# A linear-attention block and an FFN on one core: Q by seven block products, some of them among the K/V tiles

## The chip, the core and the metric

The kernel runs on one core of a Trainium2 chip. The metric is the device time of one execution in microseconds; the time before is the median of three runs.

## The reference

Two blocks read the same layer-normalised input `xn` (2048 tokens, 1024 features), and the second gates the first.

```python
xn = layernorm(x)                                   # (1, 2048, 1024), no scale or bias
q, k, v = split_heads(xn @ wqkv)                    # 32 heads of 32
phi = lambda t: where(t > 0, t + 1, exp(t)) + 1e-6
pq, pk = phi(q), phi(k)
kv = einsum("bhsd,bhse->bhde", pk, v)               # one 32x32 matrix a head, over all tokens
z  = pk summed over the tokens
o  = (pq @ kv) / (pq . z + 1e-6)
s  = o @ wo
g  = silu((silu(xn @ w_gate) * (xn @ w_up)) @ w_down)
return x + s * g
```

K and V of all 2048 tokens must be known before the first `o`; Q is needed only from there on.

## The kernel before

**Layout.** Tokens go in 16 tiles of 128 rows (`i`), in 4 blocks of 512 (`b`) and, in the FFN, in 2 passes of 1024 (`p`). `xnT[p]` holds `xn` transposed, features on the partitions, in fp16. The first 8 tiles are transposed by PE (`emit_T`, L305), blocks 2 and 3 through DRAM with a DMA transpose (`emit_A2_block`, L341).

**K and V.** `emit_B(i, c)` (L375) multiplies one token tile with a chunk of 512 columns of the K/V weights, 8 matmuls of 128x512; chunks 0 and 1 are K, chunks 2 and 3 are V. `emit_phi` (L123) makes phi of a 512-wide chunk in fp32: an exp and a relu on ACT, an addition of 1e-6 on Pool or DVE (L128), and min and add in one DVE instruction (L129). `emit_C(i)` (L379) adds the tile's `pk`-by-`v` products into three PSUM tiles `kvz`, 8 small matmuls.

**Q.** `emit_Q(b, g)` (L144) is one group of 128 output features for one block: 8 matmuls of 128x512 (L150) and an `emit_phi` into `pqT`. There are 4 x 8 groups, so 256 matmuls.

**Output of the attention.** `emit_ND(b, t)` (L510) multiplies `pqT` with the masked `KVZ`, 8 small matmuls into three PSUM tiles, and divides on DVE. When the four tiles of a block are done, `emit_OT(b)` (L537) stores the block to `o_dram` in one DMA and reads it back with a DMA transpose into `oT`. `emit_S(b, t, cc)` (L543) multiplies with `wo`, 8 matmuls of 128x512 each, 32 such calls.

**Order.** Up to tile 2 an order written by hand holds for PE, DVE, ACT and Pool. After that a scheduler places the instructions, in about the order of the source: all eight Q groups of block 0 after the last K/V tile, then a queue `fq` gives two pieces of work (L563) after every `emit_ND`: the Q groups of blocks 1 to 3 first, then `emit_S` of the blocks that are through. PSUM has three buffers for `psA` (`kvz`, later `nd_ps`), three for `psB` (`kv_ps`, `q_ps`, `s_ps`) and two for `psC`.

**FFN.** Each of its groups is a 2x2 block product done with seven products of half size, 28 matmuls instead of 32. `Group` (L608) runs it in parts: `part_a` (M3 into X, M4 into Y), `part_b` (M1 into Z, M5 onto X, M2 onto Y), `part_c` (N7 onto X, N6 onto Y); ACT copies X, and DVE makes the running sum u and the two differences u - X and u - Y. The operands are sums of blocks of `xnT` (five of them a pass, `xs`, L750) and of the weights (`sum_w`, L761). The first `sum_w` calls stand inside the FFN's own order.

Of the kernel before, what the change touches and what calls it, by code (L numbers as in the profile page):

```python
# [21 lines left out]
def kernel(  # L22
# [37 lines left out]
    PE_T_BLOCKS = min(2, NB)  # L60
# [10 lines left out]
    wgu = ctx.enter_context(tc.tile_pool(name="wgu", bufs=4, side=RIGHT))  # L71
    ps12 = ExitStack()
    psA = ps12.enter_context(tc.tile_pool(name="psA", bufs=3, space=PSUM))
    psB = ps12.enter_context(tc.tile_pool(name="psB", bufs=3, space=PSUM))
    psC = ps12.enter_context(tc.tile_pool(name="psC", bufs=2, space=PSUM))
# [40 lines left out]

    def blk_rows(t_dram, b):
        return t_dram[b * TB:(b + 1) * TB, :]
# [4 lines left out]
    def emit_phi(work, t_ps, dst, W, eng=None):  # L123
        e_t = work.tile([P, W], FP32, name="e_t", tag="e_t")
        ex = nc.scalar.activation(out=e_t[:], in_=t_ps, func=ACT.Exp)
        r_t = work.tile([P, W], FP32, name="r_t", tag="r_t")
        nc.scalar.activation(out=r_t[:], in_=t_ps, func=ACT.Relu)  # L127
        (eng or nc.vector).tensor_scalar(out=r_t[:], in0=r_t[:], scalar1=EPS, scalar2=None, op0=ALU.add)  # L128
        nc.vector.scalar_tensor_tensor(out=dst, in0=e_t[:], scalar=1.0, in1=r_t[:],  # L129
                                       op0=ALU.min, op1=ALU.add)  # L130
        return ex

    p12 = ExitStack()
    wqp = p12.enter_context(tc.tile_pool(name="wqp", bufs=1))
    blk12 = p12.enter_context(tc.tile_pool(name="blk12", bufs=3))
    wop = p12.enter_context(tc.tile_pool(name="wop", bufs=1))
    phiw = p12.enter_context(tc.tile_pool(name="phiw", bufs=3))

    wq_sb = wqp.tile([P, DC, D], BF16, name="wq_sb")
    wo_sb = wop.tile([P, G, D], BF16, name="wo_sb")  # L140

    pqT_tiles = {}

    def emit_Q(b, g):  # L144
        if b not in pqT_tiles:
            pqT_tiles[b] = blk12.tile([P, G, TB], BF16, name="pqT", tag="pqT")
        pqT = pqT_tiles[b]
        q_ps = psB.tile([P, TB], FP32, name="q_ps", tag="B")
        for dc in range(DC):
            nc.tensor.matmul(q_ps[:], lhsT=wq_sb[:, dc, g * P:(g + 1) * P], rhs=xn_blk_ap(b)[:, dc, :],  # L150
                             start=(dc == 0), stop=(dc == DC - 1))
        emit_phi(phiw, q_ps[:], pqT[:, g, :], TB)
# [846 lines left out]
```

## Time and profile before

| what | value |
|---|---|
| median of the runs | 766.86 us (766.53 to 766.88) |
| profiled execution, its own time | 767.05 us |
| its span (first to last instruction) | 765.3 us |
| PE busy | 753.2 us, 98% of the span |
| DVE busy | 481.3 us, 63% |
| ACT busy | 271.5 us, 35% |
| Pool busy | 81.1 us, 11% |
| first FFN matmul of the profiled execution | 251.32 us |

The profiled execution is 1.75 us longer than its span and 0.19 us longer than the median. A matmul of 512 columns shows as 379 ns, but matmuls are pipelined; how closely they follow each other is read from the start of one run of matmuls to the start of the next. A line of the timeline gives the start, the duration of the merged instructions, the engine, the source line, the operation, the tiles, the count and, in brackets, the idle time of that engine just before it with what ended it. In lines of groups the last columns are busy time, mean duration of one instruction, and idle time before them.

### The profile page before, as it was taken

Reading aid. Unit: us, or ns where it says so; the run is one execution under the profiler, and the core shown is the slowest. Engines: PE = TensorE matmul, PEld = TensorE weight load, DVE = VectorE, ACT = ScalarE, POOL = GpSimd, SP = SyncE. Lnnn points to the kernel's source line nnn. Section 1 sums busy time; section 2 is a strip of 40 time slices with the busy share of each in tenths; the row PEclk is TensorE's granted clock in tenths of the full one; section 3 lists DMA queues with packets and bytes.
Section 4 is the critical chain, followed back from the end, with each engine's and each line's share of the span. In section 5 each row is a group of like instructions: output and inputs, shape, how many; then the busy total and the mean of one; then the engine's idle time right before and its main releaser. Section 6 shows DMA issues by size and latency. Waiting matters only on the chain.

```text
span 765.3 us, 9974 instructions
## 1 busy us (share of the span) xinstructions
PE 753.2 (98%) x3760; PEld 354.8 (46%) x3796; DVE 481.3 (63%) x955; ACT 271.5 (35%) x473; POOL 81.1 (11%) x89
## 2 busy tenths in 40 slices
PE   9999999999999999999999999999999999999997
PEld 3445444455544444444444444444444444444454
DVE  7777112699760677677876778767655654455454
ACT  3444444555333443433334333334433111111111
POOL 3133434000000000000000000000000221212220
PEclk9999999999999999999999999999999999999999
DMA  9545362015561155553555535453959944454300
GB/s 319 179 144 171 69 150 70 1 56 150 167 193 69 51 150 158 158 172 96 166 151 154 170 104 173 144 144 106 319 179 331 363 180 179 179 174 148 118 28 27
DMA packets 127087, 115.98 MB, mean 152 GB/s; under 512 B 28864, under 2 KB 107840, under 8 KB 125760
## 3 DMA queue, kind: packets, MB, share of 16 engines
q1 hardware_dynamic: 126752, 114.97, 47.8%
q8 instruction: 29, 0.48, 0.3%
q10 hardware_dynamic: 288, 0.39, 0.1%
q14 instruction: 18, 0.15, 0.1%
HBM read 70.52 MB, written 38.54 MB: 143 GB/s over the span
## 4 chain that ended last, share of the span: by engine, by line
PE 95%; DVE 3%; issue 1%; POOL 0%; ACT 0%; DVEq 0%
PE X L605 28%; PE Y L605 28%; PE kv_ps L359 12%; PE Z L605 9%; PE q_ps L150 7%; PE s_ps L551 7%; DVE stats L245 1%; PE nd_ps L523 1%; PE w_ps L401 1%; PE kvz L383 1%; PE tr_ps L312 0%; DVE pk_sb L129 0%; DVE xnT L332 0%; DVE mv L260 0%; POOL lnw L288 0%
## 5 line engine op out<-in xcount | busy, mean ns | idle before, releaser
L605 PEld LDWEIGHTS <-ws_all 128*128 128x128 bf16 x1260 | 122.0, 98 | 145.7 <-DVE ws_all L764 1.7
L625 DVE TENSOR_TENSOR q<-n,Y 128x512 f32<-128x512 f32 x63 | 43.3, 687 | 133.6 <-PE Y L605 132.7
L359 PE MATMUL kv_ps<-wkv_sb,xnT 128*128 128x512 bf16 x499 | 113.4, 379 | 2.2 <-ACT r_t L127 1.0
L932 POOL TENSOR_TENSOR o_out<-y,xres 128x512 bf16<-128x512 f32 x28 | 34.1, 1218 | 576.8 <-DVE y L931 576.8
L605 PEld LDWEIGHTS <-xs 128*128 128x128 bf16 x616 | 57.9, 98 | 63.2
L359 PEld LDWEIGHTS <-xnT 128*128 128x128 f16 x512 | 49.0, 98 | 57.9 <-issue 1.6
L605 PE MATMUL Y<-xs,ws_all 128*128 128x512 f16 (+3 forms) x308 | 70.3, 360 | 0.0
L605 PE MATMUL X<-xnT,ws_all 128*128 128x512 f16 (+1 forms) x278 | 70.1, 379 | 0.2
L605 PE MATMUL Z<-xs,ws_all 128*128 128x512 f16 x224 | 57.5, 379 | 1.2 <-DVE ws_all L764 1.2
L605 PE MATMUL Y<-xnT,ws_all 128*128 128x512 f16 x224 | 57.5, 379 | 0.0
L605 PE MATMUL X<-xs,ws_all 128*128 128x512 f16 x224 | 57.5, 379 | 0.0
L150 PE MATMUL q_ps<-xnT,wq_sb 128*128 128x512 f16 x256 | 57.3, 379 | 0.0
L551 PE MATMUL s_ps<-wo_sb,oT 128*128 128x512 bf16 x250 | 55.7, 379 | 0.3
L129 DVE SCALAR_TENSOR_TENSOR pk_sb<-e_t,r_t 128x512 bf16<-128x512 f32 x32 | 21.9, 688 | 54.2 <-POOL r_t L128 54.1
L784 ACT ACTIVATE g<-cg 128x512 bf16<-128x512 f32 x56 | 35.3, 630 | 54.3 <-DVE cg L640 54.3
L631 DVE TENSOR_TENSOR u<-Z,q 128x512 f32<-128x512 f32 x63 | 43.2, 686 | 15.7 <-PE Z L605 15.7
L784 ACT ACTIVATE g<-X 128x512 bf16<-128x512 f32 x28 | 16.7, 597 | 101.3 <-PE X L605 101.3
L128 POOL TENSOR_SCALAR r_t<-r_t 128x512 f32<-128x512 f32 x26 | 39.4, 1517 | 71.1 <-ACT r_t L127 60.9
L621 ACT COPY n<-X 128x512 f32<-128x512 f32 x63 | 36.9, 585 | 28.4 <-PE X L605 28.4
L809 DVE TENSOR_TENSOR ho<-g,up 128x1024 bf16<-128x1024 bf16 x56 | 38.2, 686 | 0.5
L551 PEld LDWEIGHTS <-oT 128*128 128x128 bf16 x256 | 24.8, 98 | 29.1
L150 PEld LDWEIGHTS <-wq_sb 128*128 128x128 bf16 x256 | 24.5, 98 | 27.2
(124 smaller groups left out, 979.3 us busy)
## 6 DMA issues: line engine op xcount, KB each, us to landing
h_dram<-ho SPq DMA_DIRECT2D x56, 256.0 KB, 2.5
wg_sb<-in_B_w_gate_dram SPq DMA_DIRECT2D x14, 512.0 KB, 4.1
wu_sb<-in_B_w_up_dram SPq DMA_DIRECT2D x14, 512.0 KB, 4.6
wdr<-in_B_w_down_dram SPq DMA_DIRECT2D x14, 512.0 KB, 4.1
ws_all<-h_dram SPq DMA_DIRECT2D x4, 1792.0 KB, 8.7
wds_dram<-wdsA SPq DMA_DIRECT2D x14, 384.0 KB, 2.8
hp_a<-h_dram SPq DMA_DIRECT2D x3, 1792.0 KB, 8.8
o_dram<-o_blk SPq DMA_DIRECT2D x4, 1024.0 KB, 4.6
```

Source lines behind the costliest of these rows:

```text
L128: (eng or nc.vector).tensor_scalar(out=r_t[:], in0=r_t[:], scalar1=EPS, scalar2=None, op0=ALU.add)
L129: nc.vector.scalar_tensor_tensor(out=dst, in0=e_t[:], scalar=1.0, in1=r_t[:], op0=ALU.min, op1=ALU.add)
L150: nc.tensor.matmul(q_ps[:], lhsT=wq_sb[:, dc, g * P:(g + 1) * P], rhs=xn_blk_ap(b)[:, dc, :], start=(dc == 0), stop=(dc == DC - 1))
L359: mm = nc.tensor.matmul(kv_ps[:], lhsT=xn_tok_ap(i)[:, dc, :], rhs=wkv_sb[:, dc, c * CW:(c + 1) * CW], start=(dc == 0), stop=(dc == DC - 1))
L551: nc.tensor.matmul(s_ps[:], lhsT=oT[:, c, ttok], rhs=wo_sb[:, c, cc * CW:(cc + 1) * CW], start=(c == 0), stop=(c == G - 1))
L605: marks["mm"] = nc.tensor.matmul(acc[:, 0:c1 - c0], lhsT=lhs(k), rhs=rhs(k)[:, c0:c1], start=(first and k == 0), stop=(k == n - 1), skip_g ...
L621: nc.scalar.copy(out=n[:], in_=self.X[:])
L625: nc.vector.tensor_tensor(out=self.q[:], in0=n[:], in1=self.Y[:], op=ALU.add)
L631: nc.vector.tensor_tensor(out=self.u[:], in0=Z[:], in1=self.q[:], op=ALU.add)
L784: nc.scalar.activation(out=self.g[:, i, j * TB:(j + 1) * TB], in_=src, func=ACT.Silu)
L809: nc.vector.tensor_tensor(out=self.ho[:, i], in0=self.g[:, i], in1=self.up[:, i], op=ALU.mult)
L932: (nc.vector if last else nc.gpsimd).tensor_tensor(out=self.o_out[:, i, cs], in0=t[:], in1=self.xres[:, i, cs], op=ALU.add)
```

## The change

Q is made by the FFN's method. `QGroup(p, m)` stands for 256 output features and 1024 tokens: 28 matmuls in parts a, b and c as in the FFN, and a part d for phi. There are 4 groups in each of 2 passes, so 224 matmuls. The sums `xs` of both passes and the sums of the Q weights are made earlier, spread among the K/V tiles by a queue `later`. The groups of pass 0 stand inside the K/V tiles 9, 11, 13 and 15; those of pass 1 follow after the last K/V tile, with the four `emit_ND` of block 0 among them.

Phi becomes bf16 and 1024 wide: exp and relu write bf16 tiles `e_t` and `r_t` of 1024 columns from the pool `phiw` (three buffers each), and `emit_phi(eng, ...)` is one tensor_scalar (min with 1, add 1e-6) and one tensor_tensor. It runs on DVE, except for the second row of each group of pass 1, which goes to Pool. In the built program all four of these second rows of pass 1 lie at the same address (`e_t` and `r_t` alike).

PSUM has five buffers for `psB` and none for `psC`. The `xn` tiles, the Q groups' outputs `pqT` and the transposed `o` of blocks 2 and 3 take memory that the FFN's sums, the weight buffers and `wq_sb` use at other times. A block's `o` is stored by tile, four DMAs, before the DMA transpose. An order written by hand now holds on PE, DVE, ACT and Pool up to the FFN; SP's is still set by the scheduler. The FFN's first weight sums stand among the last `emit_S`. The FFN itself is not changed.

```diff
-    psB = ps12.enter_context(tc.tile_pool(name="psB", bufs=3, space=PSUM))
-    psC = ps12.enter_context(tc.tile_pool(name="psC", bufs=2, space=PSUM))
+    psB = ps12.enter_context(tc.tile_pool(name="psB", bufs=5, space=PSUM))
...
+    def xsum_ops(p):
+        b11, b12 = xnT[p][:, 0:HD, 0:TB], xnT[p][:, 0:HD, TB:2 * TB]
+        b21, b22 = xnT[p][:, HD:DC, 0:TB], xnT[p][:, HD:DC, TB:2 * TB]
+        return [lambda k=k, u=u, v=v, op=op: nc.vector.tensor_tensor(out=XS[p][:, k], in0=u, in1=v, op=op)
+                for k, (u, v, op) in enumerate(((b21, b11, ALU.subtract), (b12, b22, ALU.subtract), (b11, b22, ALU.add),
+                                                (b21, b22, ALU.add), (b11, b12, ALU.add)))]
...
+    def block_operands(w, ws):
+        ws = ws.rearrange("p (k c) -> p k c", k=HD)
+        return {"M4": lambda k: w[:, HD + k, P:2 * P], "M3": lambda k: w[:, k, 0:P],
+                "M1": lambda k: ws[:, k, 0:P], "M5": lambda k: ws[:, k, P:2 * P], "M2": lambda k: ws[:, k, 2 * P:3 * P],
+                "N7": lambda k: ws[:, k, 3 * P:4 * P], "N6": lambda k: ws[:, k, 4 * P:5 * P]}
...
+    def emit_exp_relu(e, r, t):
+        nc.scalar.activation(out=e, in_=t, func=ACT.Exp)
+        nc.scalar.activation(out=r, in_=t, func=ACT.Relu)
+    def emit_phi(eng, dst, e, r):
+        eng.tensor_scalar(out=e, in0=e, scalar1=1.0, scalar2=EPS, op0=ALU.min, op1=ALU.add)
+        return eng.tensor_tensor(out=dst, in0=e, in1=r, op=ALU.add)
...
-    def emit_Q(b, g):
-        if b not in pqT_tiles:
-            pqT_tiles[b] = blk12.tile([P, G, TB], BF16, name="pqT", tag="pqT")
-        pqT = pqT_tiles[b]
-        q_ps = psB.tile([P, TB], FP32, name="q_ps", tag="B")
-        for dc in range(DC):
-            nc.tensor.matmul(q_ps[:], lhsT=wq_sb[:, dc, g * P:(g + 1) * P], rhs=xn_blk_ap(b)[:, dc, :],
-                             start=(dc == 0), stop=(dc == DC - 1))
-        emit_phi(phiw, q_ps[:], pqT[:, g, :], TB)
+    phiw = p12.enter_context(tc.tile_pool(name="phiw", bufs=3))
...
+    def phi_tiles():
+        return (phiw.tile([P, SP_TOK], BF16, name="e_t", tag="e_t"), phiw.tile([P, SP_TOK], BF16, name="r_t", tag="r_t"))
...
+    class QGroup:
+        def __init__(self, p, m, eng1):
+            w = wq_sb[:, :, m * FW:(m + 1) * FW]
+            self.lhs, self.rhs = block_operands(w, ws_all[:, m // 2, m % 2]), x_operands(p)
+            self.eng = (nc.vector, eng1)
+            self.out = wgu.tile([P, 2, SP_TOK], BF16, name="pqT", tag=("wg_sb" if m % 2 == 0 else "wu_sb"))
+            pqT_tiles[(p, m)] = self.out
+            self.row = {}
+        def mm(self, acc, which, first):
+            products(acc, self.lhs[which], self.rhs[which], HD, first)
...
+        def er(self, i, j):
+            if i not in self.row:
+                self.row[i] = phi_tiles()
+            return tuple(t[:, j * TB:(j + 1) * TB] for t in self.row[i])
+        def part_a(self):
+            self.X = psB.tile([P, CW], FP32, name="qX", tag="B")
+            self.mm(self.X, "M3", True)
+            self.u = qtmp.tile([P, CW], FP32, name="qu", tag="qu")
+            nc.scalar.copy(out=self.u[:], in_=self.X[:])
+            self.Y = psB.tile([P, CW], FP32, name="qY", tag="B")
+            self.mm(self.Y, "M4", True)
+            nc.vector.tensor_tensor(out=self.u[:], in0=self.u[:], in1=self.Y[:], op=ALU.add)
+        def part_b(self):
+            Z = psB.tile([P, CW], FP32, name="qZ", tag="B")
+            self.mm(Z, "M1", True)
+            nc.vector.tensor_tensor(out=self.u[:], in0=self.u[:], in1=Z[:], op=ALU.add)
+            self.mm(self.X, "M5", False)
+            emit_exp_relu(*self.er(0, 1), self.X[:])
+            self.mm(self.Y, "M2", False)
+            emit_exp_relu(*self.er(1, 0), self.Y[:])
+        def part_c(self):
+            for acc, which, i in ((self.X, "N7", 0), (self.Y, "N6", 1)):
+                self.mm(acc, which, False)
+                e, r = self.er(i, i)
+                nc.vector.tensor_tensor(out=r, in0=self.u[:], in1=acc[:], op=ALU.subtract)
+                emit_exp_relu(e, r, r)
+        def part_d(self):
+            for i in range(2):
+                emit_phi(self.eng[i], self.out[:, i, :], *(t[:] for t in self.row[i]))
...
+    ET = mybir.EngineType
+    FRONT_ORDER = {ET.PE, ET.DVE, ET.Activation, ET.Pool}
...
+        def emit_B_out(i, c):
+            kv_ps = kv_tiles.pop((i, c))
+            if c < NCC:
+                if c == 0:
+                    er_tiles[i] = phi_tiles()
+                emit_exp_relu(*(t[:, c * CW:(c + 1) * CW] for t in er_tiles[i]), kv_ps[:])
+                if c == NCC - 1:
+                    pk_tiles[i] = work.tile([P, D], BF16, name="pk_sb", tag="pk_sb")
+                    emit_phi(nc.vector, pk_tiles[i][:], *(t[:] for t in er_tiles.pop(i)))
...
+        later = deque()
+        for b in range(2, NB):
+            for t in range(TPB):
+                later.append(lambda i=b * TPB + t: emit_stats(i, parts=(0,)))
+                later.append(lambda i=b * TPB + t: (emit_stats(i, parts=(1,)), emit_aggr(i)))
+            later.append(lambda i=b * TPB: emit_rstd(i))
+            if b > 2:
+                for t in range(TPB):
+                    later.append(lambda b=b, t=t: emit_norm(b * TPB + t, xn_blk_slot(b)[:, t, :]))
+                later.append(lambda b=b: emit_xT_block(b))
+            else:
+                norm_b2 = [lambda b=b, t=t: emit_norm(b * TPB + t, xn_blk_slot(b)[:, t, :]) for t in range(TPB)]
+                norm_b2.append(lambda b=b: emit_xT_block(b))
+        pos = 2 * TPB + 1 + 4
+        later = deque(list(later)[:pos] + norm_b2 + list(later)[pos:])
+        later.extend(xsum_ops(0))
+        for m in range(NM_Q):
+            later.extend(wsum_ops(wq_sb[:, :, m * FW:(m + 1) * FW], ws_all[:, m // 2, m % 2]))
+        later.extend(xsum_ops(1))
...
+        with tc.manual_schedule(engines=FRONT_ORDER):
...
+            Q0 = 2 * TPB + 1
+            qp0 = deque(range(NM_Q))
+            for i in range(TPB, NT):
+                grp = QGroup(0, qp0.popleft(), nc.vector) if i >= Q0 and (i - Q0) % 2 == 0 and qp0 else None
+                nf = 1 if grp else 2
+                emit_B(i, 0)
+                fill(nf)
+                emit_C(i - 1)
+                if grp:
+                    grp.part_a()
+                emit_B(i, 1)
+                fill(nf)
+                if grp:
+                    grp.part_b()
+                if i == TPB:
+                    emit_T(TPB + 2)
+                emit_B(i, 2)
+                fill(nf)
+                if i == TPB:
+                    emit_T(TPB + 3)
+                if grp:
+                    grp.part_c()
+                emit_B(i, 3)
+                if grp:
+                    grp.part_d()
+                fill(nf)
+            emit_C(NT - 1)
...
+            nc.sync.dma_start(out=o_dram[r0:r0 + P, :], in_=o_sb[:])
+            if t == TPB - 1:
+                nc.sync.dma_start_transpose(out=oT_of(b), in_=blk_rows(o_dram, b))
...
+        with tc.manual_schedule(engines=FRONT_ORDER):
+            qs = [QGroup(NPASS - 1, m, nc.gpsimd) for m in range(NM_Q)]
+            qs[0].part_a()
+            emit_KVZ()
+            qs[0].part_b()
+            emit_ND(0, 0)
+            for m in range(1, NM_Q):
+                qs[m].part_a()
+                qs[m - 1].part_c()
+                emit_ND(0, m)
+                qs[m - 1].part_d()
+                qs[m].part_b()
+            qs[-1].part_c()
+            qs[-1].part_d()
+            nd = deque((b, t) for b in range(1, NB) for t in range(TPB))
+            ns = 0
+            for b in range(NB):
+                for t in range(TPB):
+                    for cc in range(NCC):
+                        if nd and (nd[0][0] == 1 or ns % 2 == 0):
+                            emit_ND(*nd.popleft())
+                        emit_S(b, t, cc)
+                        ns += 1
+                    if (b, t) == (NB - 1, 0):
+                        sum_w(0, 0)
+                        sum_w(0, 1)
+                if b == 0:
+                    load_w(0, after=marks[("S", 0, TPB - 1, 0)])
+                    load_w(1, after=marks[("S", 0, TPB - 1, 0)])
+                if b == 1:
+                    load_w(2, after=marks[("S", 1, TPB - 1, 0)])
+    p12.close()
+    ps12.close()
...
-        sum_w(0, 0)
-        sum_w(0, 1)
```

In `emit_T`, `emit_rstd` and `emit_norm` only the tiles' places and the grouping change: tiles 4 to 7 get their mean and variance in pairs, and the iterations for 1/sqrt all run on Pool.

## The prediction

> **What bounds the kernel now.** I read the page's busy shares and chain first, then PE's waits, PE's timeline from the start to the first FFN matmul, the groups of Pool and DVE, and the DMA issues. Busy shares and chain:
>
> ```profile
> PE 753.2 (98%) x3760; PEld 354.8 (46%) x3796; DVE 481.3 (63%) x955; ACT 271.5 (35%) x473; POOL 81.1 (11%) x89
> ...
> PE X L605 28%; PE Y L605 28%; PE kv_ps L359 12%; PE Z L605 9%; PE q_ps L150 7%; PE s_ps L551 7%; DVE stats L245 1%; PE nd_ps L523 1%; PE w_ps L401 1%; PE kvz L383 1%; PE tr_ps L312 0%; DVE pk_sb L129 0%; DVE xnT L332 0%; DVE mv L260 0%; POOL lnw L288 0%
> ```
>
> PE is the bound in every stage, and Q is 7% of the chain. So a removed matmul counts in full, and so does every new wait of PE. PE's largest waits, as out, line, releaser: sum, count, longest in us:
>
> ```profile
> PE tr_ps L312 <- DVE xn L296: 1.6, 1, 1.6
> PE Z L605 <- DVE ws_all L764: 1.2, 1, 1.2
> PE kv_ps L359 <- ACT r_t L127: 1.0, 2, 0.6
> ```
>
> Nothing there exceeds 1.6 us; the scheduler keeps PE fed. PE's timeline:
>
> ```profile
> 1.17 6.06 PE L401 MATMUL w_ps<-warm 128*128 128x512 bf16 x14 [1.17 <-DVE warm L90]
> ...
> 151.08 3.62 PE L150 MATMUL q_ps<-xnT,wq_sb 128*128 128x512 f16 x16
> ...
> 154.53 0.63 PE L523 MATMUL nd_ps<-KVZ,pqT 128*128 128x132 bf16 x8
> 155.00 3.61 PE L150 MATMUL q_ps<-xnT,wq_sb 128*128 128x512 f16 x16
> ...
> 254.40 1.04 PE L605 MATMUL Z<-xs,ws_all 128*128 128x512 f16 x4 [1.19 <-DVE ws_all L764]
> ```
>
> From 151.08 to 154.53 are 16 matmuls: 0.216 us each. From there to 155.00 an `emit_ND` takes 0.47.
>
> **The part with one answer: gains.** 256 Q matmuls become 224: 32 x 0.216 = 6.9. Five `psB` buffers and the new front order take away PE's early gaps, 0.65 + 0.40 at two K/V tiles (releaser ACT r_t) and 1.62 before a transpose: 2.7. The FFN's first sums now stand ahead of the last `emit_S`, so the 1.19 goes: 1.2. Together 10.8. The Q groups of pass 0 lie inside K/V tiles; their sums of `xn` and weights and their phi run on DVE, busy 63% of the time, and I cost them at nothing while K/V matmuls cover them. ACT needs 12.6 us for two K/V tiles and a group, where PE has 19.9. If that cover fails, each pass-0 group may lose up to 0.65, a gap like the one seen, 2.6 in all. I take 0. The load of `wo_sb`, moved behind K/V, takes 8.8 to landing and has the whole pass-1 stage before it.
>
> **The pass-1 Q groups.** Here PE order is fixed, and it runs against a loop. A group's second row of phi goes to Pool, and all four of these rows use one tile `e_t` and one `r_t`. So ACT cannot write the exp of Y of group m until Pool has finished group m-1, and N6(m), which adds onto Y, waits for that exp and relu. The prices:
>
> ```profile
> L128 POOL TENSOR_SCALAR r_t<-r_t 128x512 f32<-128x512 f32 x26 | 39.4, 1517 | 71.1 <-ACT r_t L127 60.9 <-DVE lnw L288 6.1 <-DVE stats L245 4.1
> L932 POOL TENSOR_TENSOR o_out<-y,xres 128x512 bf16<-128x512 f32 x28 | 34.1, 1218 | 576.8 <-DVE y L931 576.8
> ...
> L128 DVE TENSOR_SCALAR r_t<-r_t 128x512 f32<-128x512 f32 x38 | 15.9, 420 | 8.1 <-ACT r_t L127 8.0
> L809 DVE TENSOR_TENSOR ho<-g,up 128x1024 bf16<-128x1024 bf16 x56 | 38.2, 686 | 0.5
> ```
>
> Pool takes 1.49 (its undisturbed rows) and 1.22 for 512 fp32 columns. By elements, less a fixed part of 0.19 (its smallest row), 1024 columns cost 2.79 + 2.25 = 5.04; by bytes, as bf16 halves them, 1.49 + 1.22 = 2.7. No row shows Pool in bf16 at 1024. I take elements, since L932 already writes bf16 and is no nearer to half of L128; beside DVE the first row reaches 1.80, so the high end is about 7.
>
> [...]
>
> The loop: Pool 5.04; exp and relu of Y, 0.49 apart on ACT, 1.08; queued on ACT behind them the copy of X of the next group, 0.5; on DVE the u that waits for this copy and then u - X, 0.69 each; exp, relu and exp on ACT, 1.6, which give Pool its next input; handovers 0.4. That is 10.0 a group. PE's work between N6(m-1) and N6(m) is 28 x 0.216 + 0.47 = 6.5, and 4.8 for the last group, which has no part a behind it. The waits of N6: group 1 2.7 (0.8 of slack is left from the start), group 2 3.5, group 3 5.2. Queued behind N6 on PE is everything, `emit_ND` of block 1 and S(0,0,0).
>
> S(0,0,0) also waits for the first transposed block:
>
> ```profile
> s_dram<-s_sb SPq DMA_DIRECT2D x16, 256.0 KB, 2.1
> ...
> oT<-o_dram SPq DMA_TRANSPOSE x4, 6.0
> ```
>
> From the end of part c of group 2: DVE's queue 1.6, the division of ND(0,3) 2.1, store and SP 2.2 (the 256 KB row), transpose 6.0, handover 0.2: 12.1. PE's work in that time is ND 0.47, part b 2.6, part c 1.73, ND(1,0) 0.47: 5.27. So 6.8 is lost there, of which group 3's 5.2 is a part. In the old order Q groups of 3.45 filled this time. Stage loss: 2.7 + 3.5 + 6.8 = **13.0**. With Pool price p it is 13.0 + 2(p - 5.04): 8.3 at 2.7 and 16.9 at 7. When Pool does not bind, the transpose alone still costs 6.1: the DVE queue is then shorter, 11.35 - 5.27.
>
> **The S stage.** SP's order is the scheduler's: the transpose of block 1 is queued behind stores of S and of block 2, that of block 3 behind a 512 KB weight load. Four stores of 256 KB replace one of 1024 KB (4.6 to landing), which shortens the way for the last tile to 2.1. I take 0.3 for `emit_ND`'s pace with DVE, 1.2 for block 1 (0 to 3), 0 for block 2 (margin 1.2; up to 4 if a transpose takes the 8.7 of the `xnT` row instead of 6.0) and 1.5 for block 3 (0.5 to 3): **3.0**. Bounds 0.8 to 10, the high end unlikely as it needs every collision.
>
> **The clock.** PE now stands idle for 3 to 7 us several times. In the trace the longest idle time inside is 1.62, and PEclk reads 9 throughout, so no row shows what such an idle time does. The nearest row is the start: 14 cold matmuls in 6.06, 0.43 each, against 0.216, so a full restart costs up to 3.0. A cold clock also fills part of the next wait with slower matmuls, which costs nothing. I take half of one restart, **1.5** (0 to 9). [...]
>
> **Sum.** -10.8 + 13.0 + 3.0 + 1.5 = +6.7. On the profiled execution, 767.05 + 6.7 = 773.75. That execution lies 0.19 above the median, so the forecast is **773.6 us**.
>
> **Rivals.**
>
> *Pool paced by bytes (other side).* At 2.7 the stage loses 8.3; with S at its low 0.8 and no clock cost, -10.8 + 8.3 + 0.8 = -1.7, 765.2. Against it: L932's output is bf16 and gains nothing. For it: DVE's 1024 bf16 columns at 686 ns are fast beside its 420 ns for 512 in fp32. Break-even is a Pool price of 3.5 with the low terms, 1.9 with mine. Range 764 to 769; chance 0.22, of which faster 0.14, same 0.05, slower 0.03.
>
> *The clock drops in each wait.* Three or four restarts at 3.0 instead of 1.5: +7.5 to +10.5, so 781 to 784, with the other high ends up to 787. Chance 0.18, all slower.
>
> *Only the transpose binds.* If the scheduler's waits let ACT go ahead of Pool, the loss is 6.1 and the sum -10.8 + 6.1 + 3.0 + 0 = -1.7, again 765.2. The shared tile speaks against it; it is counted in the first rival's 0.22.
>
> **How the numbers follow.** My own case, 769 to 780, has 0.60: faster 0.01, same 0.03, slower 0.56. With the rivals: faster 0.15, same 0.08, slower 0.77; 0.2% is 1.5 us, about what a measurement of this kernel can tell from no change. The range of 8 in 10 goes from **766** (half of the first rival) to **782** (the smaller half of the second).
>
> **What would show it.** Right: 224 Q matmuls; no gaps at K/V tiles and before the FFN's Z; waits of 2.7, 3.5 and about 5 of N6 on ACT, which itself waits on Pool for `e_t`; Pool's rows at about 2.8 and 2.25; S(0,0,0) about 1.6 behind a DMA; the first FFN matmul at about 258 or 259, for 251.32 before. Wrong in price: Pool's pair under 3.5, and N6's waits under 2. Wrong in mechanism: the profile shows no wait on Pool in this stage, or the gaps lie in the K/V tiles instead, where I counted none. Clock: PEclk below 9 in the slices from 150 to 200 us.

## The result, and the profile after

| | before | changed |
|---|---|---|
| median | 766.78 us (766.53 to 766.88, 6 runs) | 783.54 us (781.59 to 784.54, 6 runs) |
| span of the profiled execution | 765.3 us | 781.7 us |
| first FFN matmul | 251.32 us | 268.94 us |

The change makes the kernel slower: 1.0217 times the time before, 95% interval 1.0204 to 1.023. The forecast was 773.6 us in 766 to 782. The sign was right, the size was not: the span grew by 16.4 us where the sum said 6.7.

The page: busy times, and the rows of PE and of its granted clock in 40 slices (19.5 us each).

```profile
PE 754.5 (97%) x3764; PEld 354.0 (45%) x3764; DVE 476.9 (61%) x892; ACT 276.2 (35%) x481; POOL 73.9 (9%) x118
...
PE   8999999985987999999999999999999999999997
...
PEclk9999999999999999999999999999999999999999
```

PE is busy for 1.3 us more than before although it has 32 matmuls less (the counts of records do not show that: the trace before has, for example, 499 records for the 512 K/V matmuls, the one after all 512): some matmuls became slower. Apart from the first and the last slice its row has holes only from about 156 to 254 us. PEclk stays at 9 (90% or more) in every slice, so the page does not show the slower matmuls; the last section reads the granted clock in shorter windows.

PE's waits (out, line, releaser: sum, count, longest in us):

```profile
PE qY L131 <- ACT r_t L187: 10.1, 3, 4.4
PE s_ps L662 <- DMA wq_sb<-o_dram: 5.4, 2, 3.7
PE s_ps L662 <- DMA oT<-o_dram: 1.5, 1, 1.5
PE nd_ps L635 <- DVE o_sb L645: 1.3, 1, 1.3
PE qX L131 <- ACT r_t L187: 1.2, 1, 1.2
```

The first line is N6 (onto `qY`), three times, the last N7 of group 3 (onto `qX`). `wq_sb<-o_dram` are the transposes of blocks 2 and 3, whose `oT` lies in the memory of `wq_sb`; `oT<-o_dram` is block 1. The old waits of K/V tiles for ACT, and of Z on `ws_all`, are gone; of the 1.6 ahead of a transpose 0.9 is left, at another one (`tr_ps` on `ws_all`).

PE's timeline at these places:

```profile
167.41 1.03 PE L131 MATMUL qX<-xs,ws_all 128*128 128x512 f16 x4
171.59 1.86 PE L131 MATMUL qY<-xs,ws_all 128*128 128x512 f16 x4 [3.14 <-ACT r_t L187]
173.25 1.08 PE L635 MATMUL nd_ps<-KVZ,pqT 128*128 128x132 bf16 x8
...
182.33 1.02 PE L131 MATMUL qY<-xs,ws_all 128*128 128x512 f16 x4 [2.46 <-ACT r_t L187]
...
193.07 1.86 PE L131 MATMUL qY<-xs,ws_all 128*128 128x512 f16 x4 [4.44 <-ACT r_t L187]
194.73 1.08 PE L635 MATMUL nd_ps<-KVZ,pqT 128*128 128x132 bf16 x8
195.61 3.48 PE L662 MATMUL s_ps<-wo_sb,oT 128*128 128x512 bf16 x8
198.93 0.63 PE L635 MATMUL nd_ps<-KVZ,pqT 128*128 128x132 bf16 x8
...
253.45 15.64 PE L662 MATMUL s_ps<-wo_sb,wq_sb 128*128 128x512 bf16 x64 [3.74 <-DMA wq_sb<-o_dram]
268.94 1.03 PE L131 MATMUL X<-xs,wg_sb 128*128 128x512 f16 x4
```

S(0,0,0) begins at 195.61, and its 8 matmuls take until 198.93, 0.415 us each instead of 0.216. The 64 matmuls from 253.45 take 15.49 instead of 64 x 0.216 = 13.8. In the windows from 172 to 174, 192 to 198 and 254 to 256 us the granted clock is 0.50. ACT and Pool in the pass-1 stage:

```profile
170.45 0.60 ACT L186 ACTIVATE e_t<-qY 128x512 bf16<-128x512 f32 x1 [4.31 <-POOL pqT L191]
```

```profile
164.59 3.63 POOL L190 TENSOR_SCALAR e_t<-e_t 128x1024 bf16<-128x1024 bf16 x1 [97.35 <-ACT e_t L186]
168.30 2.12 POOL L191 TENSOR_TENSOR pqT<-e_t,r_t 128x1024 bf16<-128x1024 bf16 x1
175.33 3.63 POOL L190 TENSOR_SCALAR e_t<-e_t 128x1024 bf16<-128x1024 bf16 x1 [4.92 <-ACT e_t L186]
```

ACT's exp of Y begins when Pool has finished the group before (168.30 + 2.12 = 170.42), N6 follows at 171.59, and Pool's next row starts 10.74 us after its last. The chain of the profile, taken in this window, runs through exactly these: Pool, ACT, DVE, ACT, Pool.

Where the 16.4 us are, counted at 0.216 us a matmul and 0.47 an `emit_ND`:

| stage | forecast | measured | how |
|---|---|---|---|
| 32 matmuls less | -6.9 | -6.9 | 7 groups of 32 in the profile, 224 |
| K/V tiles to the end of the last C | -2.7 | -3.1 | 133.78 less 2 Q matmuls before; 155.26 less 116 after |
| FFN, first matmul to the end of the span | -1.2 | -1.2 | 513.98 before, 512.76 after |
| pass-1 Q to S(0,0,0) | +13.0 | +14.7 | 155.26 to 195.61, work 25.7 |
| S stage without slower matmuls | +3.0 | +9.5 | 195.61 to 268.94, work 60.5, less 3.3 |
| slower matmuls that count | +1.5 | +3.3 | 1.6 at S(0,0,0), 1.7 at S(3,0,0) |
| sum | +6.7 | +16.3 | |

The gains came as forecast. The losses were larger by 10.0 us, of which 6.5 are the S stage's; all but a wait of `emit_ND` for DVE were in places foreseen.

### The profile page after: what moved, and what is told of

Its sections match the earlier page's. It is cut to its first block, busy times and chain, and to the rows that moved or that the text cites. A ratio compares the mean times of both kernels' runs of the same rounds, so it can differ in the third digit from the quotient of the medians.

```text
span 781.7 us, 9960 instructions
## 1 busy us (share of the span) xinstructions
PE 754.5 (97%) x3764; PEld 354.0 (45%) x3764; DVE 476.9 (61%) x892; ACT 276.2 (35%) x481; POOL 73.9 (9%) x118
## 4 chain that ended last, share of the span: by engine, by line
PE 76%; issue 13%; DMA 4%; POOL 3%; DVE 2%; ACT 1%; SPq 0%; POOLq 0%; DVEq 0%
PE X L131 28%; PE Y L131 27%; PE Z L131 9%; PE kv_ps L430 5%; PE s_ps L662 4%; DMA wq_sb<-o_dram 2%; POOL e_t L190 1%; DMA o_dram<-o_sb 1%; DMA oT<-o_dram 1%; POOL pqT L191 1%; ACT e_t L186 1%; DMA xp<-in_A_x_dram 1%; DVE stats L323 1%; PE nd_ps L635 0%; PE tr_ps L398 0%
## 5 line engine op out<-in xcount | busy, mean ns | idle before, releaser
L131 PEld LDWEIGHTS <-ws_all 128*128 128x128 bf16 x1420 | 138.1, 98 | 175.1 <-issue 14.0
L430 PE MATMUL kv_ps<-wkv_sb,xnT 128*128 128x512 bf16 x512 | 115.6, 379 | 0.5 <-DVE xnT L413 0.5
L666 ACT CAST s_sb<-s_ps 128x512 bf16<-128x512 f32 x32 | 18.6, 586 | 54.1 <-PE s_ps L662 43.7
L1008 DVE TENSOR_TENSOR y<-y,s_in 128x512 f32<-128x512 f32 x31 | 22.2, 716 | 21.1 <-ACT y L1002 15.8
L662 PE MATMUL s_ps<-wo_sb,wq_sb 128*128 128x512 bf16 x128 | 29.8, 395 | 5.4 <-DMA wq_sb<-o_dram 5.4
L131 PEld LDWEIGHTS <-wg_sb 128*128 128x128 bf16 x224 | 21.9, 98 | 26.4
L131 PEld LDWEIGHTS <-wu_sb 128*128 128x128 bf16 x224 | 21.9, 98 | 26.4
L662 PE MATMUL s_ps<-wo_sb,oT 128*128 128x512 bf16 x128 | 30.8, 393 | 1.5 <-DMA oT<-o_dram 1.5
```

The lines of the kernel that those rows point to most:

```text
L131: marks["mm"] = nc.tensor.matmul(acc[:, 0:c1 - c0], lhsT=lhs(k), rhs=rhs(k)[:, c0:c1], start=(first and k == 0), stop=(k == n - 1), skip_g ...
L430: mm = nc.tensor.matmul(kv_ps[:], lhsT=xn_tok_ap(i)[:, dc, :], rhs=wkv_sb[:, dc, c * CW:(c + 1) * CW], start=(dc == 0), stop=(dc == DC - 1))
L662: mm = nc.tensor.matmul(s_ps[:], lhsT=oT[:, c, ttok], rhs=wo_sb[:, c, cc * CW:(cc + 1) * CW], start=(c == 0), stop=(c == G - 1))
L666: nc.scalar.copy(out=s_sb[:, cc * CW:(cc + 1) * CW], in_=s_ps[:])
L1008: nc.vector.tensor_tensor(out=t[:], in0=t[:], in1=self.s_in[:, i, cs], op=ALU.mult)
```

## Experiments

All start from the changed kernel; the last three put several edits together. The kernel before had medians between 766.85 and 766.94 us in the same runs.

### e1_dve_phi: the second row of phi on DVE

```diff
-            qs = [QGroup(NPASS - 1, m, nc.gpsimd) for m in range(NM_Q)]
+            qs = [QGroup(NPASS - 1, m, nc.vector) for m in range(NM_Q)]
```

> The second row of phi of the four pass-1 Q groups goes from Pool to DVE; nothing else changes. Theory (the loop through Pool and the shared tile sets the pace of the pass-1 groups, period 10.74 us in the changed kernel's trace): DVE does the row in 0.42 + 0.69 = 1.1 us instead of Pool's 5.75, so N6's three waits (3.14, 2.46, 4.44 us) and N7's 1.20 shrink to under 1 us each. DVE then has about 7.1 us of work a group where PE has 6.5, and S(0,0,0), so far hidden behind N6's wait, waits 5 to 7 us for the first transposed block. First S matmul about 36 us after the end of the last pass-0 group instead of 43.6; the kernel gets 6 to 8 us faster than the changed one: 776 us (774 to 779). Rival (DVE or ACT, not Pool, sets the pace): N6 still waits 2 us or more in every group and the time stays within 3 us of 783.5.

Measured: 776.43 us (774.92 to 778.03), 7.1 less. PE's waits:

```profile
PE s_ps L662 <- DMA oT<-o_dram: 6.6, 2, 5.7
PE s_ps L662 <- DMA wq_sb<-o_dram: 5.7, 2, 4.0
...
PE qX L131 <- ACT r_t L187: 1.0, 1, 1.0
...
PE qY L131 <- ACT r_t L187: 0.4, 1, 0.4
```

N6's 10.1 us shrink to 0.4, and S(0,0,0) now waits 5.70 for the transpose that N6's waits had covered. One engine name in one line was worth 7 us, and no more, since the next wait lay behind it.

### e2_own_tiles: Pool keeps the row, in tiles of its own

```diff
...
+    phi_pool = {}
+    def phi_own():
+        return tuple(phi_pool["p"].tile([P, SP_TOK], BF16, name=n, tag=n) for n in ("e_o", "r_o"))
...
+            self.own = p > 0 and m % 2 == 1
...
-                self.row[i] = phi_tiles()
+                self.row[i] = phi_own() if i == 1 and self.own else phi_tiles()
...
+        phi_pool["p"] = p2.enter_context(tc.tile_pool(name="phio", bufs=1))
```

> Pool keeps the second row of phi, but the tiles of this row no longer share one address: groups 1 and 3 of pass 1 get a pair of tiles of their own. (The constant tile of the warm-up is put into memory of the later sums of xn to make room.) Theory (the shared tile closes the loop; Pool's price alone, 5.75 us a group against 6.5 us of PE work, does not bind): N6's waits vanish or stay under 0.5 us, Pool's two instructions still take 3.6 and 2.1 us, and S(0,0,0) waits 5 to 6 us for the first transpose: 8 to 9 us less than the changed kernel, 775 us (773 to 778). Rival (Pool is too slow in itself, or its work slows DVE): N6 still waits for 2 us or more and the gain is under 4 us.

Measured: 776.29 us (774.52 to 776.54). N6 waits nowhere; Pool's rows are unchanged, and S(0,0,0) waits 5.48:

```profile
170.82 3.63 POOL L190 TENSOR_SCALAR e_o<-e_o 128x1024 bf16<-128x1024 bf16 x1 [0.67 <-ACT e_o L186]
174.53 2.12 POOL L191 TENSOR_TENSOR pqT<-e_o,r_o 128x1024 bf16<-128x1024 bf16 x1
```

Pool idles 0.67 us instead of 4.92 between rows: 5.8 us of Pool per group fit under PE's 6.5. So the cost needs both, a slow engine and a tile that the next group gets again: a fast engine on the shared tile (e1) gains 7.1 us, the slow engine with a second tile 7.25.

### e8_one_op: one operation instead of two on Pool

```diff
+        if eng is nc.gpsimd:
+            eng.tensor_scalar(out=e, in0=e, scalar1=1.0, scalar2=None, op0=ALU.min)
+        else:
+            eng.tensor_scalar(out=e, in0=e, scalar1=1.0, scalar2=EPS, op0=ALU.min, op1=ALU.add)
-        eng.tensor_scalar(out=e, in0=e, scalar1=1.0, scalar2=EPS, op0=ALU.min, op1=ALU.add)
```

> The changed kernel, but Pool's tensor_scalar does one operation (min with 1) instead of two (min with 1, add 1e-6); in these four rows phi lacks its 1e-6. Theory (my price of 2.79 us was scaled from L128, which does one operation, and the second operation is what makes it 3.63): the instruction takes about 2.8 us, the period of the loop through Pool falls from 10.74 to about 9.9, N6's waits fall by about 0.8 each, and the time by 1.7 to 2.5 us: 781.5 us (780.5 to 782.5). Rival (it is the form, 1024 columns in place and in bf16, that costs 3.63): the instruction still takes 3.5 us or more and the time stays within 0.7 us of 783.5.

Measured: Pool's instruction took 2.8 us as forecast, the time only 1.0 less, 782.56 us (781.21 to 783.78).

```profile
L191 POOL TENSOR_SCALAR e_t<-e_t 128x1024 bf16<-128x1024 bf16 x4 | 11.2, 2809 | 111.8 <-ACT e_t L186 111.8
```

My scaling by elements was right (2.79 from L128's 1.49); what I scaled does one operation, and the changed kernel's instruction does two. A gain of 1.0 is not clear of the spread of the runs, and it is below the forecast range. In the profiled execution N6's waits fell from 10.1 to 7.4 us, but S(0,0,0) now waits 1.39 for its transpose: the loop through Pool and the transpose end nearly together.

### e7_early_only: block 0's emit_ND earlier, the tile still shared

```diff
             qs[0].part_b()
             emit_ND(0, 0)
-            for m in range(1, NM_Q):
-                ...
+            qs[1].part_a(); qs[0].part_c(); emit_ND(0, 1); qs[0].part_d()
+            qs[1].part_b(); emit_ND(0, 2)
+            qs[2].part_a(); qs[1].part_c(); emit_ND(0, 3); qs[1].part_d()
+            ...
```

The added lines are joined here.

> The changed kernel with one difference: the four emit_ND of block 0 stand behind parts b0, c0, b1 and c1; Pool's rows share their tile as in the changed kernel. Theory (the wait for the first transpose and the loop through Pool overlap in time, and the loop ends last): N6's waits add up to about the same 11 us, S(0,0,0) starts at the same time within 1 us, and the time is that of the changed kernel: 783 us (781.5 to 784.5). Rival (the two waits add): 3 us or more are gained, under 780.5 us.

Measured: 781.24 us (780.48 to 782.24), 2.3 less, between the two. The experiment was not pure: the loop runs only twice, and N6 waits two times, 5.1 us in all, instead of three. Pool's starts 165.60, 176.34 and 187.09 keep the period of 10.74, and the fourth row follows without a wait at 193.00. That fits a second row of group 3 that lies at another address with this order; the traces do not show addresses. S(0,0,0) starts at 191.25, 4.4 us earlier than in the changed kernel, but PE then waits 3.8 us for DVE's divisions, so neither theory describes the run. That the two waits overlap is shown by e1 and e2, where taking the one away uncovers the other.

### e4_fill: matmuls on zeros in three of PE's waits

```diff
+    def fill_pe(n):
+        f_ps = psB.tile([P, TB], FP32, name="f_ps", tag="B")
+        for _ in range(n):
+            nc.tensor.matmul(f_ps[:], lhsT=warm[:, 0:P], rhs=warm[:], start=True, stop=True)
...
+            self.fill = {1: 11, 3: 16}.get(m, 0) if p > 0 else 0
...
+                if which == "N6" and self.fill:
+                    fill_pe(self.fill)
...
+                        if (b, t, cc) == (NB - 1, 0, 0):
+                            fill_pe(14)
```

> Matmuls on zeros, whose result nobody reads, are put into three of PE's waits of the changed kernel: 11 ahead of N6 of group 1 (wait 3.14 us), 16 ahead of N6 of group 3 (4.44 us) and 14 ahead of S(3,0,0) (3.74 us). They fit into the waits, so without an effect of idleness the time does not change. Theory (after an idle time of about 3 us and more PE runs at half rate for 3 to 4 us, seen as matmuls 0.415 us apart instead of 0.216): the matmuls behind the three places run at 0.216 again. At group 1 this gains nothing since the loop through Pool sets the pace; at group 3 and the first S it gains up to 2.8 us, less what the first transpose then binds, so about 2; at S(3,0,0) it gains 1.7. Together 3.5 to 4 us less: 779.8 us (779 to 781). Rival (the slower matmuls come from something else, for example transfers or weight loads at that time): they stay slower and the time stays within 0.7 us of 783.5.

Measured: 780.65 us (779.86 to 781.03), 2.9 less.

```profile
189.42 3.62 PE L208 MATMUL f_ps<-warm 128*128 128x512 bf16 x16
193.25 1.02 PE L131 MATMUL qY<-xs,ws_all 128*128 128x512 f16 x4 [0.22 <-ACT r_t L187]
...
195.38 1.90 PE L670 MATMUL s_ps<-wo_sb,oT 128*128 128x512 bf16 x8 [0.64 <-DMA oT<-o_dram]
...
248.34 3.19 PE L208 MATMUL f_ps<-warm 128*128 128x512 bf16 x14
251.51 13.99 PE L670 MATMUL s_ps<-wo_sb,wq_sb 128*128 128x512 bf16 x64
265.33 1.03 PE L131 MATMUL X<-xs,wg_sb 128*128 128x512 f16 x4
```

Behind the filled waits all matmuls run at 0.216 again: the last 64 take 13.82 instead of 15.49. The slower matmuls come from PE's idleness. Where nothing was filled, ahead of N6 of group 2, the wait is 3.60 and the matmuls behind it are slow (the four of Z take 1.70 us, 184.53 to 186.23, for 0.86). At N6 of group 1 nothing is gained, since the loop sets the pace (N6 of group 2 begins at 182.50, in the changed kernel at 182.33). So slow matmuls inside a stage that waits anyway cost nothing, and ahead of S they cost 1.6 and 1.7.

### e3_late_loads: the FFN's first weight loads later

```diff
+                        if (b, t, cc) == (0, 3, 0):
+                            load_w(0, after=marks[("S", b, t, cc)])
+                        if (b, t, cc) == (2, 0, 0):
+                            load_w(1, after=marks[("S", b, t, cc)])
+                        if (b, t, cc) == (3, 0, 0):
+                            load_w(2, after=marks[("S", b, t, cc)])
-                if b == 0:
-                    load_w(0, ...); load_w(1, ...)
-                if b == 1:
-                    load_w(2, ...)
...
-                load_w(m + PREF)
+                load_w(m + PREF, after=marks[("S",) + (3, 0, 1)] if m == 0 else None)
```

> Only the places of the FFN's first weight loads change: those of group 1 go behind S(2,0,0), of groups 2 and 3 behind S(3,0,0) and S(3,0,1); with this the sums of group 1 no longer stand among the emit_ND of blocks 2 and 3 in DVE's order. Theory (the waits of the S stage come from these loads: the transposes of blocks 2 and 3 and the stores before them queue or share the DMA engines with them, and DVE waits for one of them ahead of emit_ND): emit_ND's wait of 1.26 us and block 2's 1.70 us go, block 3's 3.74 us falls under 1.5 us, and with it the 1.7 us of slower matmuls behind that wait: 5 to 8 us less, 777 us (775 to 779); block 1's 1.45 us stays. Rival (store and transpose are just too long for the room that PE's order leaves, with or without loads): block 3 still waits over 2.5 us and the gain is under 3 us.

Measured: 779.53 us (777.41 to 780.95), 4.0 less: a part. What happened in the changed kernel is seen on SP and DVE there:

```profile
217.91 4.05 SPq L179 DMA_DIRECT2D wu_sb<-in_B_w_up_dram  x1
222.05 1.61 SPq L650 DMA_DIRECT2D o_dram<-o_sb  x1
...
224.27 0.38 SPq L650 DMA_DIRECT2D o_dram<-o_sb  x1
...
229.22 3.90 SPq L652 DMA_TRANSPOSE wq_sb<-o_dram  x1
```

```profile
225.58 0.43 DVE L152 TENSOR_TENSOR ws_all<-wg_sb 128x512 bf16<-128x512 bf16 x1 [3.67 <-DMA wg_sb<-in_B_w_gate_dram]
```

The issue of one load holds SP for 4.05 us (what it waits for the trace does not tell), two stores of block 2 stand behind it, the transpose is issued another 4.6 us behind the last of them (224.65 to 229.22), 3.6 of which SP waits for the store to land, and DVE stands 3.67 us in front of the sums of group 1 with the division of ND(3,0) behind it. With the loads moved, block 2 waits 0.61 instead of 1.70, and `emit_ND`'s wait is gone. But block 3 still waits 2.91, and the reason is on DVE again:

```profile
237.16 0.42 DVE L152 TENSOR_TENSOR ws_all<-wg_sb 128x512 bf16<-128x512 bf16 x1 [4.48 <-DMA wg_sb<-in_B_w_gate_dram]
```

My edit had moved the sums of group 1 only as far as ahead of ND(3,3), whose matmuls end at 235.24; the store of that tile is issued at 240.57. The gain of 4.0 is above the rival's 3, the wait of 2.91 is the rival's. So the run did not tell the theory from its rival, and e11 does.

### e11_loads_sums: the loads last, and no sum ahead of an emit_ND

```diff
+                        if (b, t, cc) == (0, 3, 0):
+                            load_w(0, after=marks[("S", b, t, cc)])
+                        if (b, t, cc) == (3, 0, 0):
+                            load_w(1, after=marks[("S", b, t, cc)])
+                        if (b, t, cc) == (3, 1, 0):
+                            load_w(2, after=marks[("S", b, t, cc)])
...
                         sum_w(0, 1)
+                        sum_w(1, 0)
+                        sum_w(1, 1)
...
-                load_w(m + PREF)
+                load_w(m + PREF, after=marks[("S",) + (3, 2, 0)] if m == 0 else None)
...
-                if p == 0 and m + 1 < NM:
+                if p == 0 and 1 < m + 1 < NM:
```

> The changed kernel with the FFN's first loads out of the way of all stores and transposes (group 0 behind S(0,3,0), group 1 behind S(3,0,0), groups 2 and 3 behind S(3,1,0) and S(3,2,0)), and the sums of group 1 written behind those of group 0, so that no sum stands ahead of an emit_ND on DVE. In e3_late_loads one such place was left: there DVE waited 4.48 us for a load of group 1 in front of the division of ND(3,3), and the store of that tile was issued 5.3 us after its matmuls had ended. Theory (loads and the sums behind them cost the S stage its waits; by themselves division, store and transpose need about 11 us and PE has 10.8): no wait for o_sb, block 2 under 0.7 us, block 3 under 1.2 us and no slower matmuls behind it; block 1's 1.45 falls to about 1. With 1.7 + 1.3 + 2.5 + 1.7 + 0.5 us gained the time is 775.8 us (774.5 to 777.2). Rival (store and transpose are too long for PE's order in any case): block 3 waits 2.5 us or more, as in e3_late_loads, and the time stays above 778.

Measured: 774.86 us (774.38 to 775.36), 8.7 less than the changed kernel.

```profile
234.32 0.63 PE L635 MATMUL nd_ps<-KVZ,pqT 128*128 128x132 bf16 x8
234.79 10.52 PE L662 MATMUL s_ps<-wo_sb,wq_sb 128*128 128x512 bf16 x47
245.82 13.99 PE L662 MATMUL s_ps<-wo_sb,wq_sb 128*128 128x512 bf16 x63 [0.51 <-DMA wq_sb<-o_dram]
259.65 1.03 PE L131 MATMUL X<-xs,wg_sb 128*128 128x512 f16 x4
```

SP's rows show where block 3's time went. In the changed kernel:

```profile
241.51 0.38 SPq L650 DMA_DIRECT2D o_dram<-o_sb  x1
...
247.51 3.79 SPq L652 DMA_TRANSPOSE wq_sb<-o_dram  x1
```

In this run:

```profile
236.96 0.34 SPq L650 DMA_DIRECT2D o_dram<-o_sb  x1
...
239.55 4.12 SPq L652 DMA_TRANSPOSE wq_sb<-o_dram  x1
```

The block's last store is issued 6.0 us ahead of its transpose in the changed kernel and 2.6 here. SP issues nothing there from 244.29 to 247.51 and waits 3.1 us for the store to land. Three loads are issued around that store (239.09, 239.58 and 243.88), none here. So at block 3 it is the late landing that costs, and not the loads' place in SP's queue; that the loads make it late fits the two runs.

From ND(3,3) to the transposed block are 11.5 us (234.32 to 245.82), for 14.7 in the changed kernel (238.73 to 253.45), and the 64 matmuls behind it run at 0.216. Blocks 1, 2 and 3 wait 0.87, 0.53 and 0.51. With the loads and the sums out of the way the whole S stage loses 3.8 us (195.36 to 259.65, work 60.5), 1.1 of slower matmuls at S(0,0,0) included. Loads and sums were moved together, so their shares are not separated, and the FFN behind does not get longer (512.75 us from its first matmul to the end of the span, for 512.76).

### e10_sp_order: SP's order by hand

```diff
-        with tc.manual_schedule(engines=FRONT_ORDER):
+        with tc.manual_schedule(engines=FRONT_ORDER | {ET.SP}):
...
-                    load_w(0, after=marks[("S", 0, TPB - 1, 0)])
-                    load_w(1, after=marks[("S", 0, TPB - 1, 0)])
+                    load_w(0)
+                    load_w(1)
...
-                    load_w(2, after=marks[("S", 1, TPB - 1, 0)])
+                    load_w(2)
```

> The changed kernel with SP's order of issues written out too, in the order of the source, from the last K/V tile to the FFN: each transpose stands straight behind the last store of its block, ahead of the stores of S that came first before; the weight loads keep their places among the S calls. Theory (not SP's queue but the loads themselves cost the waits of the S stage: they delay stores and transposes on the DMA engines, and DVE waits for one of them): block 1's wait falls from 1.45 to about 1, blocks 2 and 3 and emit_ND's wait for DVE stay as they are, 0 to 1.5 us less than the changed kernel: 782.8 us (782 to 784). Rival (the place in SP's queue is the cost): blocks 2 and 3 together wait under 3 us instead of 5.4, and 3 us or more are gained, as in e3_late_loads.

Measured: 787.33 us (784.05 to 788.60), slower than the changed kernel, which neither theory had. The profiled execution is the fastest of the four (784.05), so the trace shows only a part. In it block 1 no longer waits, and blocks 2 and 3 wait 3.10 and 5.41 instead of 1.70 and 3.74; both loads of group 3 (L177 and L179) are issued at 241.33 and 242.27, ahead of the last transpose at 247.32, where the changed kernel issues one of them. This is against the rival, and it fits the loads as the cost, but that this order moves one more load ahead of the transpose I had not seen. How a load's cost at block 2 divides between SP's issue and the landing of the stores stays open, and so does what the three slower executions lose.

### e5_early_o and e6_all: the repairs together

e5 adds to e2 a different order of PE, e6 adds to e5 the later loads (behind S(0,3,0), S(1,3,0), S(2,3,0), S(3,0,0)).

```diff
             qs[0].part_b()
             emit_ND(0, 0)
-            for m in range(1, NM_Q):
-                ...
+            qs[1].part_a(); qs[0].part_c(); emit_ND(0, 1)
+            qs[1].part_b(); emit_ND(0, 2)
+            qs[2].part_a(); qs[1].part_c(); emit_ND(0, 3)
+            qs[0].part_d(); qs[1].part_d()
+            qs[2].part_b(); qs[3].part_a(); qs[2].part_c(); qs[2].part_d()
+            qs[3].part_b(); emit_ND(1, 0); qs[3].part_c(); emit_ND(1, 1); qs[3].part_d()
...
```

The added lines are joined here; what e5 takes over from e2, and e6's loads, are not shown again.

> The tiles of their own for Pool's row as in e2_own_tiles, and beside it PE's order: the four emit_ND of block 0 stand closer together, behind parts b0, c0, b1 and c1 of the pass-1 groups instead of b0, c0, c1 and c2, and the first two of block 1 stand ahead of S(0,0,0), around part c of the last group, so that all later emit_ND come two S calls earlier. Theory (what is left in e2_own_tiles are waits for store and transpose, because PE has too little work of another kind behind the last emit_ND of a block: 5.3 us at block 0): now PE has about 11 us of it at block 0, so S(0,0,0)'s wait falls from 5.48 to under 1.5 us and its 1.6 us of slower matmuls go; block 1's 0.8 us goes; block 3's 4.1 us falls under 1 us, and its 1.7 us of slower matmuls go. 761.8 us (760 to 764), 14 us less than e2_own_tiles and faster than before the change. Rival (DVE cannot keep up with four divisions in two groups: it is about 3.5 us behind at ND(0,3)): S(0,0,0) still waits 3 us or more, or PE waits for DVE ahead of an emit_ND; 766 us or more.

> As e5_early_o, and the FFN's first weight loads placed so that each follows a transpose: group 0 behind S(0,3,0), group 1 behind S(1,3,0), groups 2 and 3 behind S(2,3,0) and S(3,0,0). Theory: the waits that e3_late_loads took away (1.3 us of emit_ND on DVE, about 1 us at block 2, about 1 us at block 3) go here too; PE has no wait over 1 us from the last K/V tile to the FFN, all matmuls there are 0.216 us apart, and the whole front gains what the 32 fewer matmuls (6.9 us), the early gaps (2.7 us) and the FFN's wait (1.2 us) are worth: 10.8 us less than before the change, plus at most 3 us of small waits: 758.5 us (756 to 761). Rival (the sums of gains was wrong, for instance because the 28 matmuls of a group are not paced at 0.216 us beside K/V tiles): over 763 us although the waits are gone.

Measured: e5 763.62 us (763.31 to 765.16), ratio to before 0.9962 (0.9948 to 0.9975); e6 762.2 us (761.49 to 763.02), ratio 0.9939 (0.9927 to 0.9952). Both are a little faster than the kernel before, and e5 is in its range. The waits for blocks 0 and 1 are gone, and no slow matmuls are left, but e6 missed its range by 1.2 us, with PE waiting for DVE:

```profile
PE nd_ps L642 <- DVE o_sb L652: 2.4, 2, 1.6
```

This is the rival of e5: DVE has no idle time over 0.31 us from 157 to 193 us and comes late to the divisions of block 1.

### e9_relief: less for DVE ahead of block 1

The difference is shown against e6.

```diff
-            qs[2].part_d()
             qs[3].part_b()
             emit_ND(1, 0)
             qs[3].part_c()
-            emit_ND(1, 1)
-            qs[3].part_d()
...
+            nd_at = (0, 2, 3, 5, 6, 8, 9, 11, 12, 14, 15)
...
-                        if nd and (nd[0][0] == 1 or ns % 2 == 0):
+                        if ns in nd_at:
                             emit_ND(*nd.popleft())
+                        if ns == 3:
+                            qs[2].part_d()
+                            qs[3].part_d()
```

> As e6_all, but DVE gets less to do ahead of block 1's emit_ND: phi of groups 2 and 3 goes behind ND(1,3), and PE does S(0,0,0) and S(0,0,1) between ND(1,1) and ND(1,2); the later emit_ND follow at two in three S calls. Theory (what e6_all missed of its forecast, 762.2 for 758.5, is DVE: it has no idle time from 157 to 193 us, and PE waits 2.4 us for o_sb, plus about 2 us of smaller delays of the same kind): PE's waits for o_sb fall under 1 us and the S of block 1 waits for its transpose under 1.5 us; 2 to 3.5 us less than e6_all: 759.5 us (758.3 to 760.8). Rival (the rest of the miss is spread over the front and not DVE's backlog): under 1 us is gained.

Measured: 758.39 us (758.0 to 759.1), 3.8 less than e6 and a little more than expected; ratio to before 0.989, interval 0.9875 to 0.9904. What PE still waits for, the longest and the last of the list:

```profile
PE w_ps L473 <- DVE xs L91: 1.2, 1, 1.2
PE qX L131 <- ACT r_t L187: 0.8, 1, 0.8
PE s_ps L669 <- DMA wq_sb<-o_dram: 0.6, 1, 0.6
...
PE nd_ps L642 <- DVE pqT L191: 0.5, 1, 0.5
```

With the same arithmetic as the change, the time is 25.2 us below the changed kernel's and 8.5 below the time before. Most of the forecast gains of 10.8 can be had; the order, the places of the loads and two tiles decided whether they showed.

## Why the prediction was wrong in size

**Gains: right.** 10.8 forecast, 11.2 measured, each term within 0.4.

**Pass-1 Q groups: right mechanism, one price too low.** The loop through the shared tile is what bound (e1, e2). The formula 13.0 + 2(p - 5.04) holds: Pool's pair takes 5.83 from start to end, so 14.6, and 14.7 was measured; the period of 10.0 with 0.79 more is 10.79, and 10.74 was measured. The term that failed is the tensor_scalar, 2.79 for 3.63, because the row it was scaled from does one operation (e8). The three waits came as 3.14, 2.46 and 1.20 + 4.44, for 2.7, 3.5 and 5.2; the second is short because 1.6 us of slower matmuls fill a part of the same turn (in e4, where the first wait is filled, it is 3.60). The wait of 1.6 of S(0,0,0) behind a DMA did not come: PE's slow matmuls filled it (1.2 us at N6 of group 3 and `emit_ND`; at full rate, in e4, 0.64 of it shows). The third rival, only the transpose binds, is out: ACT did wait for Pool, 4.31 us at group 1. The first rival, Pool paced by bytes, is out as well: with one operation 1024 columns in bf16 take 2.8, nearly twice the 1.49 of 512 in fp32. One sum is wrong: with my terms the break-even price of Pool is 1.7, not 1.9; the forecast does not use it.

**S stage: the step that failed.** I took 1.2, 0 and 1.5 for blocks 1, 2 and 3 and 0.3 for `emit_ND`'s pace, 3.0 in all. Measured were 1.45, 1.70 and 3.74, a wait of 1.26 for DVE that I had not listed, and about 1.4 us of pace and small delays (0.45 of it at ND(3,1), where DVE frees the three `nd_ps` one by one and the granted clock is 1.00): 9.5. The mis-sized term is the FFN's weight loads and the sums behind them: I gave them 1.5 at block 3 alone, and e11, which moves them out of the way, brings the stage down to 2.7 without slower matmuls, about what I had forecast with them. Block 2's margin of 1.2 was none, since the stores of its tiles are queued on SP behind the issue of a load. The sum has no term for the sums of group 1 on DVE, which wait 3.67 us for a load with the division of ND(3,0) behind them.

**Clock: right mechanism, half the price.** 1.5 forecast, 3.3 measured on the path, from two places with 8 slow matmuls each. I had expected slower matmuls mostly inside waits; that held for N6 of group 1 (e4), not for S. The second rival's number, 781 to 784, holds the measured time by chance: its mechanism gives only 3.3 of the 16.4. My sign for it, PEclk below 9, could not show in slices of 19.5 us; the distance from start to start did, and so does the clock in short windows.

## What to carry to other kernels

When a slow engine takes over a step, look in the built program at where its tiles lie: a tile that it holds for 6 us and that the next iteration gets again at the same address turns its latency into everybody's pace (here 10.74 us a group where PE has 6.5 of work), and a second tile was worth as much here as a faster engine (7.25 us and 7.1). For every store and transpose, compare the time from the last producer to the first reader with the work that the fixed order puts between them, and ask of each load nearby what it delays: here moving prefetches for the next stage, and the sums that wait for them, gained 8.7 us. A change that loses may hold its gain still: here order, places of loads and two more tiles for the same work were worth 25 us.

## What the runs showed of the hardware

Pool's tensor_scalar on 1024 bf16 columns takes 2.8 us with one operation and 3.63 with two, where DVE's takes 0.42 with two.

PE's slow matmuls (0.415 us) come with a granted clock of 0.50. A row of this view gives a window and its length, then busy time and count of PE, PEld, DVE, ACT and Pool, the granted clock, and the DMA engines' share and GB/s. N6 of group 1 in the changed kernel:

```profile
168.10:171.51 3.41, 0.34 (x2) 0.06 (x1) 0.00 (x0) 1.06 (x3) 2.23 (x2) 1.00 0.00 0
171.51:174.92 3.41, 3.33 (x14) 1.72 (x14) 2.61 (x7) 2.03 (x5) 0.00 (x0) 0.50 0.00 0
```

The same place in e3, after the same wait of 3.14 us:

```profile
167.05:170.46 3.41, 1.46 (x7) 0.59 (x6) 0.32 (x1) 0.00 (x0) 3.33 (x2) 1.00 0.05 17
170.46:173.87 3.41, 2.22 (x17) 1.27 (x17) 1.76 (x3) 2.00 (x4) 0.02 (x1) 1.00 0.00 0
```

The changed kernel's granted clock is 0.50 in three stretches ahead of the FFN: 171.51 to 174.92 us, 191.99 to 198.81 and 253.43 to 256.84; between them, and from 256.85 to 275, it is 1.00. The first and the third begin within the last 0.1 us of waits of 3.14 and 3.74 us, the second within the wait of 4.44; behind the wait of 2.46, at 182.33, the clock is 1.00. The length of a wait alone does not decide: behind one of 2.28 us at N6 of group 1 in e8 the four matmuls of Z take 1.71 us (173.22 to 174.93), behind the 3.14 in e3 0.86 (172.98 to 173.84). What else decides was not shown. A stretch of 3.41 us at 0.50 leaves 0.91 in a slice of 19.5 us, which is why the page's PEclk shows nothing.
